# Attention and wave mixing on one core: k and v of three batches in nine-token runs, one batch's norms by square root, and a new order of the program

## The chip, the cores and the metric

The kernel runs on one core of one Trainium2 chip. Its engines work side by side, each through its own instructions in order: PE (matrix products, with PEld for the loading of the stationary operand), DVE (VectorE), ACT (ScalarE), POOL (GpSimd) and SP (SyncE, which here only issues transfers). DMA engines move data between device memory and the core's SBUF; products land in PSUM. The metric is the device time of one execution in microseconds, lower being better. A difference of less than 2% is counted as the same.

## The reference

Eight batches, eight heads, 576 tokens, 64 numbers a head; C = 512 channels.

```python
kv  = np.einsum('bhsd,bhse->bhde', k, v)          # a 64x64 matrix for each head
out = np.einsum('bhsd,bhde->bhse', q, kv)
rms = np.sqrt(np.mean(out * out, axis=-1, keepdims=True) + 1e-06)
x   = out / rms * g_norm                          # then heads side by side: (8, 576, 512)

theta  = x @ w_theta
zr, zi = x * np.cos(theta), x * np.sin(theta)
y = np.einsum('ts,bsd->btd', w_tok_r, zr) + np.einsum('ts,bsd->btd', w_tok_i, zi)
u = x + y
result = u + np.maximum(u @ w_ch, 0.0)
```

All inputs and the output are float32.

## The kernel before

**Tiling.** A batch's 576 tokens are four full tiles of 128 rows (token 4p + j on partition p for tile j, so that a partition's four tokens are one run in memory) and a tail of 64 tokens, in which two halves of the heads or channels share the 128 partitions. NT = 5 counts them, TL = 64 is the tail.

**Stages of a batch.** Names in brackets are those of tasks and tiles.

- k and v come in as float32, `kt` and `vt` [128, 8 heads, 5, 64], two buffers each (NKV = 2), by `heads_in` (runs of four tokens, 1 KB) and `tails_in` (single tokens, 256 bytes). q comes in over POOL as float16.
- `kv_piece` makes the kv matrices: for a pair of heads five steps, of 128 rows each, for either head. The first head's result stands on partitions 0 to 63 of a PSUM tile, the second's on 64 to 127. `kv_out` copies them into block-diagonal float16 tiles (`kbd`).
- q is transposed (`qps`, then a copy to `qT`; from batch 4 on by DMA) and multiplied with `kbd` (`raw`).
- The norm: `square` on ACT, `sums` on DVE (`ss`, the epsilon is in a ninth column of the tile), `root` on POOL (`rt`, the power -0.5), and `x_make` on DVE multiplies. Five of these chains make a batch, one for each tile.
- x is transposed (`xps`, a copy to `xD`), scaled by g (`xT`), and multiplied with the theta weight (`th`), which DVE has scaled by g beforehand (`wth`, in four pieces, `scale_theta`; `g` itself is scaled first).
- Sine and cosine: whole turns on ACT (`arg<-th`), the remainder on DVE, an absolute value on either, sine and cosine on ACT (`sc`), and z = x times both on DVE (`zm`, the tail in `zt`).
- The token mix (`y`, three parts for each of 2 x 4 blocks) uses `wT`, the two token weights transposed on PE in batch 0's time (`wps`, nine copies to `wT`). Then u (`um`, kept in the `wn` buffers), its transposes (`ups`, `us`, from batch 4 on by DMA), the channel mix (`v`), and the output (`fin`, `st`).

**What sets the order.** Nothing is scheduled while the program is built: every step is a task with a number, and `TURNS`, a table of numbers written out by hand, gives the order in which all tasks of all batches are emitted. A star takes the second engine of a task that may go to ACT or DVE; `r` and `a` stand for idle products on PE, which hold a PSUM buffer of their own. Each engine runs its share of the list in that order, and the framework adds the semaphores.

**Queues.** At the start SP issues k of batch 0, the tails of k of batch 1, g and the theta weight; ACT issues v of batch 0; POOL issues q and, behind a copy of one element of batch 0's k (`hold p`, into `gate`), the token weights. Later SP issues k and v of the other batches, the moves of z's tail, the transposes by DMA and the stores. A load of batch b into a buffer waits for the kv products of batch b - 2.

**Start of the program.** DVE fills constants and sets the unused half of each tail column to zero in all four k and v buffers. ACT loads its function table with one small sine (`warm`).

Of the kernel before, what the change touches and what calls it, by code (L numbers as in the profile page):

```python
# [32 lines left out]
0 6 39 4 3 1 31 46 r1 8 9 2 32 33* 40* 47* 24 11 10 5 a1 35 13 7 26 25 23 36 34* 48 49 37* 18 20 67  # L33
41 68 38 203 22 19 21 30 42 60 61* 50 204 51 53 62 r1 r1 54 55 63 56 43 44 57 58 12 14 52 17 64 r16
69 45 15 16 59 65 29 74 70 71 66 75 122 76 123 79 87 77 80 88 94 72 73 84 81 89 85 82* 90 91 95 96
a1 126 115 132 101 116 127 134 135* 92 93 28 133 128 102 108 138 129 98 86* 103 105 139 117 97 99
124 104* 125* 118 119 120 109 83* 239 240* a1 136 137 130 205 206 207 208 121 110 100 78* 131 106
107 225 140 148 211 112 210 209 226* 111 212* 141 152 232 164 165 153 113 114 142 213 201 198 200
199 154 218 149 150 227 166 214 143 215 202 216 151 167 228 219 229 230 520 27 155 217 231 168 169
170 233 144 383 384 145 156 157 220 369 146 246 370* 241 376 221 222 377* 171 147 223 247 242 243  # L40
224 158 363 248 259 249 260 261 159 364 234 235 365 262 236 263 366 264 368 390 391 250 361 360 244
362 237 172 173* 160 161 162 245 367* 163 238 177 178 371 266 372 192 193 385 251 252 386 267 174
253 373 265 374 175 387 388 256 273 254 257 274 268 375 269* 187 287 397 398 194 188 275 195 389 378
379 182 380 183* 358 356 515 359 357 514 517 516 280 392 270 288 289 393 394 271 281 277 276* 291
278 189 404 405* 381 184 521 382 399 522 555 190 282 556* 406 541 395 523 524 417 400 258 290* 292
407 525 526 255 418 283* 401 542* 527 402 518 185 272 396 293 403 179 528* 414 415* 419 279 529 409
410* 284 543 445 411 424 176 295 296 294 297 180 530 446 447 531 191 673 674 421 544 285 425 679 680
681 306 682 683 684 534 307 426 449 532 310 311 286 535* 308 302 428 545 685 675 186 412 420* 533
448 450 298 299 300 312 309 536 313 303 304 438 546 547 318 678 677 519 427* 429 416 557 562 301 319
548 320 305 431 537 538 563* 422 439 423 440 314 696 558 451 559 539 560 330 315 316 332 321 540 337  # L50
686 317 549 432 433 434 335 441* 442 443 331 333 687 322 323 324 326 327 328 688 430 336 325 561 435
436 689 676 329 564 697 575 698 565 350 690 550 338 345 582 351 347 340 551 576 699 552 444 346 583
341 413* 584 672 826 827 828 181 453 553 700 577 585 579 348 554 342 829 352 567 572 472 701 707 334
455 452 831 830 708 454 343 353 691 484 464 408* 437 578* 568 692 693 573 476 569 473 477 478 474
580 709 570 339 960 819 843 962 832 822 821 820 349 961 854 959 710 711 475 712 694 485 465 460 486
487 466 479 467 702 703 704 695 571 461 589 723 480 586 590 587 462 481 463 591 713 603 482 468 596
724 592 604 714 705 597 483 581 605 498 598 469 456 470 754 833 508 457 458 471 499* 706 607 606*
593 608 459 718 510 834 835 755 509 719 493 594 588 494 600 726 727 756 715 500 836 599 511 609 495
838 716 839 837 501 844 503 496 728 840 504* 595 729 845 601 846 841 733 966 734 967 740 968 969 505
488 735 842 730 731 741 970 971 847 720 855 848 638 639 630 631 849 742 856 758 566 489 717 344 613  # L60
736 757 732 574 721* 611 612 610 1099 1100 1101 1102 506 725* 602 642 1104 1103* 759 737 632 640 643
641 644 633 618 619 634 635 636 614 620 760 824 823 963 761 763 972 762 502 764 983 645 857 850 851
637 747 743 621 615 616 622 722 738 744 745 748 739 858 859 617 749 750* 626 627 751 752 656 628 623
624 625 661 490 629 753 746 973 657 974 852 975 491 853 781 785 769 646 786 770 782 787 783 765 984
766 767 976 964 825 788 977 662* 647 978 666 771 985 784 772 986 768 860 354 864 497 1105 862 507
196 797 355 994 197 866 987 867 868 663 894 664 773 774 789 775 873 895 896 988 870 979 865 898 897*
874 989 793 790 794 990 791 869 776 980 981 899 875 887 871 863 877 888 991 792 900 795 777 658 982
778 779 872 796 889 992 880 668 995 1000 799 901 665 492 798 902 904 876* 878 881 659 780 993 800
# [33 lines left out]
def kernel(  # L102
# [12 lines left out]
    nc = tc.nc  # L115
# [742 lines left out]
```

## Time and profile before

| | us |
|---|---|
| median of 3 runs | 225.27 |
| lowest and highest | 224.47 and 227.89 |
| the profiled execution's own time | 227.13 |
| its span, first to last instruction | 225.4 |
| first kv product on PE | 14.27 |
| first theta product on PE | 31.61 |
| last product ends, about | 220.9 |

The span is what the profile's rows are measured in; the execution's time has some 1.7 us around it. PE's busy time counts overlapping products once, so a busy PE need not be PE at its full pace: what an instruction costs a packed engine is better read from one start to the next. A transfer's time runs from its issue to the last byte's landing, queueing included.

### The profile page before, as it was taken

The numbers are of one execution on the slowest core, as the hardware profiler recorded it, in microseconds if no ns is written. First come the engines' busy times: TensorE is split into PE (matmuls) and PEld (weight loads), VectorE is DVE, ScalarE is ACT, GpSimd is POOL, SyncE is SP. The second block draws the span as 40 slices with busy tenths as digits, with TensorE's granted clock in tenths as the row PEclk, the third lists the DMA queues.
The fourth block names the chain that finished last, engine by engine and source line by source line (L and its number), as shares of the span: only waits on it lengthen the run. The fifth ranks groups of instructions, "written<-read, shape, count | busy, mean of one in ns | idle before, by whom it ended". The sixth has DMA issues, their size and how long they took to land.

```text
span 225.4 us, 5423 instructions
## 1 busy us (share of the span) xinstructions
PE 200.1 (89%) x2138; PEld 135.9 (60%) x2138; DVE 170.8 (76%) x350; ACT 144.7 (64%) x279; POOL 83.8 (37%) x78
## 2 busy tenths in 40 slices
PE   0147878999999999999999999999997999999991
PEld 0035335688755777666766578776655665755860
DVE  6006745777889969899598986889996999888562
ACT  2002447975699999975779798637998477258031
POOL 6080970007957617556151470453512501200000
PEclk9999979999999999999999999999999999999999
DMA  4999999996999399979599959579656884665424
GB/s 124 248 304 236 244 288 255 247 214 216 120 189 299 120 182 228 240 215 145 151 242 345 257 95 176 136 151 188 114 149 171 221 132 99 215 108 153 173 77 148
DMA packets 71721, 42.91 MB, mean 190 GB/s; under 512 B 38032, under 2 KB 67088, under 8 KB 71696
## 3 DMA queue, kind: packets, MB, share of 16 engines
q1 hardware_dynamic: 55680, 34.81, 60.8%
q0 software_dynamic: 14432, 6.57, 23.4%
q10 hardware_dynamic: 1584, 1.18, 1.7%
q8 instruction: 17, 0.28, 0.6%
q14 instruction: 8, 0.07, 0.1%
HBM read 33.06 MB, written 9.44 MB: 189 GB/s over the span
## 4 chain that ended last, share of the span: by engine, by line
PE 69%; DMA 12%; DVE 7%; ACT 6%; issue 2%; POOL 1%; SPq 1%; DVEq 0%
PE y L512 26%; PE th L420 11%; PE v L420 10%; PE kv L246 7%; DMA wn<-in_moe_w_tok_r_dram 7%; DMA kt<-in_k_dram 4%; PE raw L305 3%; PE xps L263 2%; PE th L423 2%; PE ups L263 2%; DVE ot L554 2%; DVE zm L489 1%; PE v L423 1%; PE qps L263 1%; DMA out_dram<-ot 1%
## 5 line engine op out<-in xcount | busy, mean ns | idle before, releaser
L343 POOL TENSOR_TENSOR rt<-ss,mhalf 128x8 f32<-128x8 f32 (+1 forms) x40 | 62.0, 1555 | 101.8 <-DVE ss L336 101.6
L512 PE MATMUL y<-wT,zm 128*128 128x256 f16 (+1 forms) x512 | 76.5, 286 | 0.7 <-DVE ot L554 0.6
L512 PEld LDWEIGHTS <-zm 128*128 128x128 f16 x512 | 47.9, 98 | 16.5 <-issue 1.6
L517 DVE SCALAR_TENSOR_TENSOR wn<-y,gcol,xT 128x320 f16<-128x320 f32 (+1 forms) x64 | 32.0, 513 | 8.1 <-PE y L512 7.4
L327 ACT ACTIVATE sqb<-raw 128x512 f32<-128x512 f32 x32 | 19.0, 596 | 28.2 <-PE raw L305 28.2
L420 PE MATMUL th<-wth,xD 128*128 128x512 f16 x128 | 34.0, 393 | 0.0
L420 PE MATMUL v<-wch,wn 128*128 128x512 f16 x128 | 31.7, 379 | 0.0
L436 ACT ACTIVATE arg<-th 128x512 f32<-128x512 f32 (+1 forms) x40 | 22.2, 555 | 14.5 <-PE th L420 8.1
L441 DVE SCALAR_TENSOR_TENSOR arg<-arg,th 128x512 f32<-128x512 f32 (+1 forms) x40 | 25.0, 630 | 7.6 <-ACT arg L436 7.3
L466 ACT ACTIVATE sc<-arg,quarter 128x512 f16<-128x512 f32 (+1 forms) x40 | 26.9, 674 | 0.8 <-DVE arg L451 0.7
L246 PE MATMUL kv<-vt,kt 128*64 128x64 f32 x640 | 23.3, 230 | 4.4 <-DMA vt<-in_v_dram 4.4
L246 PEld LDWEIGHTS kv<-vt,kt 128*64 128x64 f32 x640 | 21.0, 143 | 8.9 <-issue 3.7
L336 DVE TENSOR_REDUCE ss<-sqb 128x8 f32<-128x520 f32 x32 | 22.0, 689 | 4.5 <-ACT sqb L327 4.5
L459 ACT ACTIVATE sc<-arg 128x512 f16<-128x512 f32 (+1 forms) x40 | 23.0, 581 | 2.7 <-DVE zm L489 1.9
L353 DVE TENSOR_TENSOR x<-raw,rt 128x512 f16<-128x512 f32 x32 | 21.9, 685 | 2.3 <-POOL rt L343 2.3
L489 DVE TENSOR_TENSOR zm<-x,sc 128x1024 f16<-128x1024 f16 x32 | 21.8, 684 | 0.9 <-ACT sc L466 0.8
L512 PE MATMUL y<-wT,zt 128*128 128x256 f16 (+1 forms) x64 | 18.3, 286 | 0.6 <-DMA zt<-zf 0.6
L554 DVE SCALAR_TENSOR_TENSOR ot<-v,us 128x512 f32<-128x512 f32 (+1 forms) x28 | 16.8, 609 | 2.4 <-PE v L420 1.5
L420 PEld LDWEIGHTS <-wn 128*128 128x128 f16 x128 | 11.9, 98 | 10.9 <-issue 0.2
L405 ACT ACTIVATE xT<-xD,gcol 128x1024 f16<-128x1024 f16 (+1 forms) x18 | 16.6, 930 | 2.5 <-DMA xD<-x 2.5
L268 ACT COPY us<-ups 128x512 f16<-128x512 f16 (+1 forms) x20 | 10.5, 529 | 11.9 <-PE ups L263 8.2
L420 PEld LDWEIGHTS <-xD 128*128 128x128 f16 x128 | 11.9, 101 | 10.0 <-issue 1.9
(73 smaller groups left out, 227.1 us busy)
## 6 DMA issues: line engine op xcount, KB each, us to landing
out_dram<-ot SPq DMA_DIRECT2D x32, 256.0 KB, 2.8
vt<-in_v_dram SPq DMA_DIRECT2D x7, 1024.0 KB, 9.4
kt<-in_k_dram SPq DMA_DIRECT2D x7, 1024.0 KB, 8.2
qh<-in_q_dram POOLq DMA_DIRECT2D x7, 512.0 KB, 6.5
kt<-in_k_dram SPq DMA_DIRECT2D x2, 512.0 KB, 7.0
kt<-in_k_dram SPq DMA_DIRECT2D x8, 128.0 KB, 6.3
vt<-in_v_dram ACTq DMA_DIRECT2D x2, 512.0 KB, 14.0
zm<-in_moe_w_theta_dram SPq DMA_DIRECT2D x1, 1024.0 KB, 12.7
```

What stands on the lines that cost most here:

```text
L246: nc.tensor.matmul(t[i * D:(i + 1) * D, hp - lo, :], kt[b % NKV][:, 2 * hp + i, j, :], vt[b % NKV][:, 2 * hp + i, j, :], start=(j == 0), s ...
L336: nc.vector.reduce_sum(out=ss[:], in_=sq_sb.pop((b, j))[:], axis=AXX)
L343: nc.gpsimd.tensor_tensor(out=rt[:], in0=ss[:], in1=mhalf[:, 0:h], op=ALU.pow)
L353: nc.vector.tensor_tensor(out=x_pair[b, p][:, :, a * HC:(a + 1) * HC].rearrange("p t (h e) -> p h t e", e=D), in0=r[:].rearrange("p (h t e ...
L420: nc.tensor.matmul(t[:], piece(kc), w[:, kc, :], start=first, stop=last)
L436: nc.scalar.activation(out=arg[:, 1, :], in_=th_ps[b, j][:], func=AFT.Copy, bias=MAGIC)
L441: nc.vector.scalar_tensor_tensor(out=arg[:, 0, :], in0=arg[:, 1, :], scalar=MAGIC, in1=th_ps.pop((b, j))[:], op0=ALU.subtract, op1=ALU.sub ...
L459: nc.scalar.activation(out=sc[:, 0, :], in_=arg_sb[b, j][:, 0, :], func=AFT.Sin, bias=0.0, scale=-TURN * SHRINK,)
L466: nc.scalar.activation(out=sc_sb[b, j][:, 1, :], in_=arg_sb.pop((b, j))[:, 1, :], func=AFT.Sin, bias=quarter[:], scale=-TURN * SHRINK,)
L489: nc.vector.tensor_tensor(out=dst, in0=x.unsqueeze(1).broadcast_to((P, 2, w)), in1=sc[:], op=ALU.mult)
L512: nc.tensor.matmul(t[:, 0:hi - lo], s, wT[:, w, lo:hi], start=n == 0, stop=n == len(z) - 1)
L517: nc.vector.scalar_tensor_tensor(out=uTb[b % NUT][:, c, lo:hi], in0=y_ps.pop((b, h, c))[:, 0:hi - lo], scalar=gcol[:, 0:1], in1=xTb[b % NX ...
```

## The change

Three things change together.

**k and v of batches 0 to 2 (NINE = 3) come in nine-token runs.** 576 tokens are 64 runs of nine tokens (RUN = 9), 2304 bytes each. Even heads stand on partitions 0 to 63, odd ones on 64 to 127 (`runs_in`, one transfer for each half i). So a head's kv sum has nine steps of 64 rows in place of five of 128: 72 products a batch for 40. The tail's loads and its cleared rows go away for these batches; for the first two batches in the other form, 3 and 4, the rows are cleared later, by `kz`, on POOL or DVE. Batch 0's k and v come in four transfers each.

**Batch 0's norms (RS = (0,)) go by square root.** ACT takes the root of the sums (`square_root`) and DVE its reciprocal, in place of POOL's power. ACT's first table load is for the square root, and a second (`load_sine`) follows after the last root.

**`TURNS` is new**, for the whole program: order, engines, and 14 idle products for 22.

```diff
@@ TURNS
-0 6 39 4 3 1 31 46 r1 8 9 2 32 33* 40* 47* 24 11 10 5 a1 35 13 7 26 25 23 36 34* 48 49 37* 18 20 67
+1 3 0 2 8 4 13 a1 15 12 6 5 33 34 41 7 9 49 37 36* 42 35 43 44 38 50* 51 52 a4 57 14 19 18 17 45 16
...
+    NINE = 3
+    RS = (0,)
-    kt = [const.tile([P, H, NT, D], FP32, name=f"kt{i}") for i in range(NKV)]
+    kt = [const.tile([P, H * NT * D], FP32, name=f"kt{i}") for i in range(NKV)]
...
+    RUN = S // TL
+    def runs_of(t):
+        return t[:, 0:NHP * RUN * D].rearrange("p (m e) -> p m e", m=NHP)
...
+    def runs_in(eng, dst, src, b, i, lo, hi):
+        eng.dma_start(
+            out=runs_of(dst)[i * TL:(i + 1) * TL, lo:hi, :],
+            in_=src[b].rearrange("(m i) (p j) d -> i p m (j d)", i=2, j=RUN)[i, :, lo:hi, :],
+        )
+    def clear_tails(i, eng):
+        e = nc.vector if eng == "DVE" else nc.gpsimd
+        for t in (kt[i], vt[i]):
+            e.memset(t[TL:P, H * NJ * D:H * NT * D], 0.0)
...
     def kv_piece(b, hp, lo, n):
...
-        for j in range(NT):
+        kb, vb = kt[b % NKV], vt[b % NKV]
+        n = RUN if b < NINE else NT
+        for j in range(n):
             for i in range(2):
+                if b < NINE:
+                    half = slice(i * TL, (i + 1) * TL)
+                    ks, vs = (runs_of(x)[half, hp, j * D:(j + 1) * D] for x in (kb, vb))
...
                 nc.tensor.matmul(
-                    t[i * D:(i + 1) * D, hp - lo, :],
-                    kt[b % NKV][:, 2 * hp + i, j, :],
-                    vt[b % NKV][:, 2 * hp + i, j, :],
-                    start=(j == 0), stop=(j == NT - 1),
+                    t[i * D:(i + 1) * D, hp - lo, :], ks, vs, start=(j == 0), stop=(j == n - 1)
                 )
...
     def root(b, j):
...
-        nc.gpsimd.tensor_tensor(out=rt[:], in0=ss[:], in1=mhalf[:, 0:h], op=ALU.pow)
+        if b in RS:
+            nc.vector.reciprocal(out=rt[:], in_=rs_sb.pop((b, j))[:])
+        else:
+            nc.gpsimd.tensor_tensor(out=rt[:], in0=ss[:], in1=mhalf[:, 0:h], op=ALU.pow)
...
+    def square_root(b, j):
+        ss = sq_sb[b, j]
+        rs = work.tile(list(ss.shape), FP32, tag="rs" + ("" if full(j) else "e"),
+                       bufs=4 if full(j) else 1, name="rs")
+        nc.scalar.activation(out=rs[:], in_=ss[:], func=AFT.Sqrt)
+        rs_sb[b, j] = rs
+    def load_sine():
+        nc.scalar.activation(out=warm[:], in_=quarter[:], func=AFT.Sin)
...
-    hold = add("hold p", "POOL", lambda: hold_pool(kt[0][0:1, H - 1, 0, 0:1]), [kb])
+    hold = add("hold p", "POOL", lambda: hold_pool(kt[0][0:1, 3 * RUN * D:3 * RUN * D + 1]), k0[1])
...
+        if NINE <= b < NINE + NKV:
+            k_.append(add(f"kz {b}", "POOL|DVE", lambda e: clear_tails(b % NKV, e), old))
...
+        if b == 0:
+            sine_ready = add("warm", "ACT", load_sine, of("rs", 0))
...
-        nc.scalar.activation(out=warm[:], in_=quarter[:], func=AFT.Sin)
-        for i in range(NKV):
-            nc.vector.memset(kt[i][TL:P, :, NJ, :], 0.0)
-            nc.vector.memset(vt[i][TL:P, :, NJ, :], 0.0)
+        nc.scalar.activation(out=warm[:], in_=quarter[:], func=AFT.Sqrt)
```

How the order moves is shown at three places. In the rows below a name with a number is one buffer (`kt_64` is k's first, `kt_65` its second, `vt_66` and `vt_67` are v's, `zm_77` first holds the theta weight), and x2 means two of the kind in a row.

The first is SP's queue at the start of the program, before:

```order
L181 DMA kt_64<-in_k_dram 128x4x256
L187 DMA kt_64<-in_k_dram 64x8x64
L181 DMA kt_64<-in_k_dram 128x4x256
L187 DMA kt_65<-in_k_dram 64x8x64
L219 DMA gcol<-in_g_norm_dram 64x1 x2
L213 DMA zm_77<-in_moe_w_theta_dram 128x4x512
L187 DMA vt_67<-in_v_dram 64x8x64
L181 DMA vt_67<-in_v_dram 128x8x256
L181 DMA kt_65<-in_k_dram 128x8x256
```

And the same place after:

```order
L207 DMA kt_64<-in_k_dram 64x2x576 x4
L244 DMA gcol<-in_g_norm_dram 64x1
L238 DMA zm_77<-in_moe_w_theta_dram 128x4x512
L244 DMA gcol<-in_g_norm_dram 64x1
L207 DMA kt_65<-in_k_dram 64x4x576
L207 DMA vt_67<-in_v_dram 64x4x576 x2
L207 DMA kt_65<-in_k_dram 64x4x576
L195 DMA vt_67<-in_v_dram 128x8x256
L207 DMA vt_66<-in_v_dram 64x4x576
L207 DMA kt_64<-in_k_dram 64x4x576
```

The theta weight stands right behind batch 0's k, with half of g on either side of it; v of batch 3 (the 128x8x256 row, into the buffer of batch 1) stands ahead of v and k of batch 2.

The second is DVE in the first batch's norms, from the copies of the kv matrices on, before:

```order
L270 COPY qT<-qps 128x512
L336 TENSOR_REDUCE ss<-sqb_92 128x8
L336 TENSOR_REDUCE ss<-sqb_93 128x8
L336 TENSOR_REDUCE ss<-sqb_92 128x8
L225 TENSOR_SCALAR gcol<-gcol 128x1
L230 TENSOR_SCALAR wth<-zm_77,gcol 128x512
L353 TENSOR_TENSOR x<-raw,rt 128x4x2x64
L230 TENSOR_SCALAR wth<-zm_77,gcol 128x512
L336 TENSOR_REDUCE ss<-sqb_91 128x8
L353 TENSOR_TENSOR x<-raw,rt 128x4x2x64
```

And after:

```order
L301 COPY qT<-qps 128x512
L250 TENSOR_SCALAR gcol<-gcol 128x1
L255 TENSOR_SCALAR wth<-zm_77,gcol 128x512 x3
L367 TENSOR_REDUCE ss<-sqb_92 128x8
L255 TENSOR_SCALAR wth<-zm_77,gcol 128x512
L301 CAST kbd_74<-kv 64x2x64 x2
L367 TENSOR_REDUCE ss<-sqb_93 128x8
L375 RECIPROCAL rt<-rs 128x8
L399 TENSOR_TENSOR x<-raw,rt 128x4x2x64
L375 RECIPROCAL rt<-rs 128x8
L301 COPY qT<-qps 128x512
L367 TENSOR_REDUCE ss<-sqb_91 128x8
```

The scaling of g and of three pieces of the theta weight moved ahead of the first sum, and reciprocals stand between the sums and x.

The third is ACT from the last root to the first weight copy, after the change:

```order
L386 ACTIVATE rs<-ss 128x4
L482 ACTIVATE arg<-th 128x512
L299 COPY xD<-xps 128x256
L482 ACTIVATE arg<-th 128x512
L390 ACT_TABLE_LOAD
L390 ACTIVATE warm<-quarter 128x1
L505 ACTIVATE sc<-arg 128x512 x2
L512 ACTIVATE sc<-arg,quarter 128x512
L482 ACTIVATE arg<-th 128x512
L299 COPY wT<-wps 128x576
```

Before, the same stretch of ACT was:

```order
L436 ACTIVATE arg<-th 128x512
L268 COPY xD<-xps 128x256
L459 ACTIVATE sc<-arg 128x512
L436 ACTIVATE arg<-th 128x512
L436 ACTIVATE arg<-th 128x256
L268 COPY wT<-wps 128x576
L466 ACTIVATE sc<-arg,quarter 128x512
L268 COPY wT<-wps 128x576
```

The second table load stands between the whole turns of batch 0's second tile and its first sine. Of the nine copies of the turned token weights ACT makes four (seven before). Over the whole program DVE has 18 copies of kv matrices (10 before), 12 full copies of transposed u and none of half width (5 and 3 before), 12 of transposed x (6), 11 scalings by g (6), 5 weight copies (2) and 4 copies of transposed q (12), each taken from or given to ACT.

More of the change, by code (lines that the diff above doesn't have):

```diff
@@ L692 @@
             ss = add(f"ss{w} {b} {j}", "DVE", lambda b=b, j=j: sums(b, j), [sq], [("ss" + w, 4)])
-            rt = add(f"rt{w} {b} {j}", "POOL", lambda b=b, j=j: root(b, j), [ss], [("rt" + w, 4)])
+            rs = ss
+            if b in RS:
+                rs = add(f"rs{w} {b} {j}", "ACT", lambda b=b, j=j: square_root(b, j), [ss])
+                last["rs", b, j] = rs
+            rt = add(f"rt{w} {b} {j}", "DVE" if b in RS else "POOL", lambda b=b, j=j: root(b, j), [rs],
+                     [("rt" + w, 4)])
             new = not full(j) or a == 0
@@ L739 @@
             ab = add(f"ab{w} {b} {j}", "DVE|ACT", lambda e, b=b, j=j: even_arg(b, j, e), [ar])
[L740 removed]
+            si = add(f"si{w} {b} {j}", "ACT", lambda b=b, j=j: sine(b, j), [ar, sine_ready],
+                     [("sc" + w, 2)])
             co = add(f"co{w} {b} {j}", "ACT", lambda b=b, j=j: cosine(b, j), [ab, si])
```

147 lines of the change are left out of this document (85 added, 62 removed), and 9 rows, old and new, of the table TURNS.

## The prediction, as it was made before the changed kernel ran

> **What bounds the kernel now.** I read the page first: busy time, the span in 40 slices, the chain that ended last.
>
> ```profile
> span 225.4 us, 5423 instructions
> PE 200.1 (89%) x2138; PEld 135.9 (60%) x2138; DVE 170.8 (76%) x350; ACT 144.7 (64%) x279; POOL 83.8 (37%) x78
> PE   0147878999999999999999999999997999999991
> PE 69%; DMA 12%; DVE 7%; ACT 6%; issue 2%; POOL 1%; SPq 1%; DVEq 0%
> ```
>
> PE is full from the eighth slice on, at about 45 us, and 69% of the chain is its own work. So there are two levers: when PE gets full, and how much work it holds from then on. The busy times by stage (columns: stretch, its length, then PE, PEld, DVE, ACT, POOL busy with counts, granted clock, DMA share, GB/s), with two short DMA stretches, say what fills the start.
>
> ```profile
> 0.00:14.20 14.20, 0.60 (x4) 0.34 (x4) 3.47 (x13) 1.49 (x2) 5.75 (x16) 1.00 0.93 204
> 14.20:31.60 17.40, 13.28 (x155) 8.75 (x156) 10.38 (x24) 5.57 (x12) 11.30 (x11) 0.99 1.20 268
> 31.60:50.00 18.40, 17.23 (x198) 11.63 (x196) 11.03 (x26) 14.27 (x29) 1.12 (x2) 0.92 1.16 238
> 150.00:180.00 30.00, 28.83 (x232) 18.09 (x230) 27.13 (x55) 22.26 (x41) 12.60 (x10) 1.00 0.77 166
> 2.00:4.00 2.00, 0.00 (x0) 0.00 (x0) 1.68 (x5) 0.23 (x2) 2.00 (x4) 1.00 0.81 259
> 14.00:20.00 6.00, 4.53 (x72) 3.59 (x74) 1.91 (x6) 0.00 (x0) 2.70 (x4) 1.00 1.20 289
> ```
>
> Until 14.2 PE has 0.6 us of work: it waits for loads. The third row's clock of 0.92 over 18.4 us is about 1.5 us of PE's pace lost, and ACT is busy 14.27 of 18.4 there. The timeline gives the milestones.
>
> ```profile
> 8.48 0.38 SPq L213 DMA_DIRECT2D zm<-in_moe_w_theta_dram  x1
> 12.13 0.17 POOL L222 COPY gate<-kt 1x1 f32<-1x1 f32 x1 [7.75 <-DMA kt<-in_k_dram]
> 14.27 1.33 PE L246 MATMUL kv<-vt,kt 128*64 128x64 f32 x20 [3.24 <-DMA vt<-in_v_dram]
> 19.24 1.39 PE L246 MATMUL kv<-vt,kt 128*64 128x64 f32 x40 [1.20 <-DMA vt<-in_v_dram]
> 21.89 0.68 DVE L336 TENSOR_REDUCE ss<-sqb 128x8 f32<-128x520 f32 x1
> 22.73 6.50 POOL L343 TENSOR_TENSOR rt<-ss,mhalf 128x8 f32<-128x8 f32 x4 [6.03 <-DVE ss L336]
> 25.43 0.48 DVE L230 TENSOR_SCALAR wth<-zm,gcol 128x512 f16<-128x512 f32 x1
> 25.83 0.68 DVE L353 TENSOR_TENSOR x<-raw,rt 128x512 f16<-128x512 f32 x1
> 28.81 0.69 DVE L353 TENSOR_TENSOR x<-raw,rt 128x512 f16<-128x512 f32 x1
> 29.41 0.42 DVE L336 TENSOR_REDUCE ss<-sqe 128x4 f32<-128x260 f32 x1
> 31.61 3.33 PE L420 MATMUL th<-wth,xD 128*128 128x512 f16 x8
> 49.93 0.27 PE L512 MATMUL y<-wT,zt 128*128 128x256 f16 x1
> zm<-in_moe_w_theta_dram SPq DMA_DIRECT2D x1, 1024.0 KB, 12.7
> ```
>
> First kv product 14.27, first sum of squares 21.89, first theta product 31.61, first product with batch 0's last z (zt) 49.93. I follow the change through these.
>
> **The loads.** Batch 0's k and v are 2.36 MB before and after, in fewer and longer runs. SP's queue now holds k (1.18 MB) and then the theta weight (1.05), ACT's holds v (1.18), POOL's q (0.52 as landed). SP sends the upper halves first and ACT the lower ones, so the first kv product needs three quarters of both: 1.77 MB and about 0.35 MB of q beside it. By 4.0 us 0.52 MB are in (259 GB/s for 2 us); at the 289 GB/s of 14 to 20 us the rest takes 5.5 us. With half a microsecond to land, kv starts near 10.0. The weight lies behind it all: 4.2 MB with the first tokens, so 4.0 + 3.7/0.289 = 16.7 at 289 GB/s and nearer 15.5 if longer runs go faster; I take 16.5 where it now lands at 8.48 + 12.7 = 21.2. The tokens' gate, now 12.13, comes earlier too and hides behind that.
>
> **The kv products.** A head's sum goes from five steps of 128 rows to nine of 64, two heads side by side: 144 matmul records in a batch for 80.
>
> ```profile
> 43.79 2.55 PE L246 MATMUL kv<-vt,kt 128*64 128x64 f32 x80
> 46.27 0.40 PE L263 MATMUL qps<-ident,qh 128*128 128x128 f16 x4
> 68.42 0.56 PE th L423 x8
> 70.30 0.86 PE th L420 x4
> ```
>
> 80 records take 46.27 - 43.79 = 2.48 us, 31 ns each, so 64 more are 2.0 us a batch. That holds if two row halves run side by side as two column halves do now: eight half-width products of 256 columns take 0.56 us, four of 512, the same columns, 0.86. No row shows row halves; the bounds are 31 and, one after the other, 62 ns. I take 31, as both keep their own columns. Batch 0's extra 2.0 us falls in the start: 72 records at the cold pace of the row at 14.27 (about 53 ns after its latency) are 3.8 us, so the first half ends near 13.9. q's transposes and the second half's first piece (36 records) stand before the first raw product; with its square the first sum could start at 17.0. But DVE now scales g and three pieces of the theta weight ahead of it, so it waits for the weight: 16.5, 0.14 for g (its row is below) and three pieces at 0.40, 17.8. That is 4.1 us earlier than 21.89.
>
> **Square root for power.** From the first sum to theta it takes 9.7 us now, as four powers on POOL take 6.50 us in a row. After, a root on ACT and a reciprocal on DVE stand between. Neither is in the trace. For the durations:
>
> ```profile
> L436 ACT ACTIVATE arg<-th 128x512 f32<-128x512 f32 x32 | 19.1, 598 | 8.4 <-PE th L420 8.1
> L459 ACT ACTIVATE sc<-arg 128x512 f16<-128x512 f32 x32 | 19.9, 624 | 2.7 <-DVE zm L489 1.9 <-DVE arg L441 0.8
> L466 ACT ACTIVATE sc<-arg,quarter 128x512 f16<-128x512 f32 x32 | 23.0, 718 | 0.7 <-DVE arg L451 0.7
> L268 ACT COPY wT<-wps 128x576 f16<-128x576 f16 x7 | 4.4, 638 | 0.7 <-PE wps L584 0.6
> L268 ACT CAST kbd<-kv 64x256 f16<-64x256 f32 x24 | 8.8, 366 | 3.0 <-PE kv L246 2.7
> L441 DVE SCALAR_TENSOR_TENSOR arg<-arg,th 128x512 f32<-128x512 f32 x32 | 21.8, 684 | 7.0 <-ACT arg L436 6.6
> L489 DVE TENSOR_TENSOR zm<-x,sc 128x1024 f16<-128x1024 f16 x32 | 21.8, 684 | 0.9 <-ACT sc L466 0.8
> L823 ACT ACT_TABLE_LOAD x1 | 1.3, 1283 | 0.7 <-PEq L842 0.7
> L823 ACT ACTIVATE warm<-quarter 128x1 f32<-128x1 f32 x1 | 0.2, 203 | 0.0
> L225 DVE TENSOR_SCALAR gcol<-gcol 128x1 f32<-128x1 f32 x1 | 0.1, 144 | 0.0
> L270 DVE CAST kbd<-kv 64x256 f16<-64x256 f32 x4 | 1.7, 421 | 1.8 <-ACT kbd L268 1.7
> L270 DVE COPY us<-ups 128x512 f16<-128x512 f16 x5 | 2.1, 417 | 0.2 <-PE ups L263 0.2
> ```
>
> A root of 8 columns lies between 0.20 (one column) and 0.60 (512); the reciprocal between 0.14 and 0.42. I take 0.2 and 0.15, the rows of one column being nearest. DVE is then the path, in its own order: three sums and three x at 0.60 from start to start (28.81 to 29.41), a weight piece at 0.40 (25.43 to 25.83), two casts 0.5, three reciprocals 0.45, a copy 0.35: 5.3 us. Transposes, their copy and the hops add 1.2. Theta starts 17.8 + 6.5 = 24.3, against 31.61: **-7.3**. With the upper ends of both prices it is 25.4; with the weight at 15.5 it is 23.3.
>
> **Theta to the first zt product.** Now 18.3 us. After, ACT's row up to the last cosine is 15.3 us: five each of the three activations above (4 at full width: 7.8, the half ones 1.3), four weight copies 2.6, two q copies, an x copy and an absolute value 2.2, the second table load with its warm-up 1.5. Three weight copies and four casts go over to DVE, which has 14.7 us there by the same counting and so stays beside ACT. PE needs 15.7 us of products there at full clock, the longer kv among them, and hides too. ACT starts 1.2 after theta and z follows 0.7 behind the cosine: 17.7 with half a microsecond of gaps, **-0.6**. Bounds: 15.7 if ACT isn't waited for, 19.5 if the clock drops again.
>
> The table load is one more than before, 1.28 us in its row. The Trainium skill, ScalarE: Activation LUTs (What ACT_TABLE_LOAD costs), gives 1283 ns and a drain of 1380 ns for every change of set. Its first figure is this trace's; by its sum this stage would be 1.4 us longer, 221.2 in the end. The trace's load has nothing ahead of it, so it cannot show a drain.
>
> **The rest.** From 49.93 on the same products stand in another order, with batch 2's 64 records: **+2.0**. ACT gives casts and copies to DVE over the whole run: 10 casts at 0.42, 7 u copies and 4 x copies at 0.42, 3 weight copies and 5 scalings, less 8 q copies: some 8 us more on DVE. DVE was busy 27.13 of 30 from 150 to 180, the one long stretch where it could lead; a tenth of the run at that density makes **+0.6** (0 if PE covers it all, 8 if none). Two memsets that go to POOL hide before batch 1's powers. On SP batch 2's loads stand behind v of batch 3, which waits for batch 1's products: out at about 36.7, 3.4 MB at 268 GB/s, in at 49.9, needed near 53; 3 us are left. The last store is a half tile: **-0.2**.
>
> Sum: -7.3 - 0.6 + 2.0 + 0.6 - 0.2 = -5.5 us: span 225.4 to 219.9. The profiled execution took 227.13 with what lies around its span, so 221.6; it stood 1.86 above the median of 225.27. For the median I predict **219.8**.
>
> **Rivals.** (1) Row halves take turns. Both heads write one accumulator tile, from different row halves. Then 288 records of batches 1 and 2 cost 31 ns more, 8.9 us, and the start 2.5: 231.2, slower than before. It decides from about 16 ns a record. For it: no row shows row halves together. Against: the column halves do run together, and these keep them. The Trainium skill, TensorEngine Tiling (Array Packing), Gotcha 1, says that different row tiles cannot access the same PSUM bank simultaneously; that is this rival, and no run here shows it yet. Chance 0.09. (2) The theta weight lands no earlier than now, 21.2: DVE's first sum waits behind it to 22.5, theta starts 29.0, and 4.7 us are lost: 224.5. For it: the DMA share is above 1.1 all along, and DVE's order puts the weight first. Against: some 2,500 runs fewer ahead of it (of k and v: 3,584 now, 1,024 after). Chance 0.17. (3) DVE becomes the pace in the middle: half of its 8 us show, 223.8. For it: 27.13 of 30; against: PE's row reads 9 there too. Chance 0.14. My forecast holds the rest, 0.60, alone between 217.3 and 222.
>
> **Numbers.** Range 217.0 to 225.5: it holds the forecast and rivals 2 and 3, and leaves out rival 1 and the ends. Two per cent is about what a measurement of this kernel tells from no change: below 220.8 is faster. Faster: four fifths of the forecast and a little of rival 2 and 3, 0.51. Slower: most of rival 1, 0.07. Same: the rest, 0.42.
>
> **What would show it.** First kv near 10, first sum near 17.8 right behind the weight, theta near 24.3, first zt product near 42; kv pairs at 31 ns a record; no power on POOL in batch 0; a second table load of 1.28 us. The forecast fails if kv records take over 45 ns, if DVE's first sum waits past 20, or if PE shows gaps behind DVE after 50.

## The result, and the profile after

| | before | after |
|---|---|---|
| median, beside each other | 225.39 us (4 runs, 224.47 to 227.89) | 232.49 us (4 runs, 231.75 to 232.88) |
| ratio after to before, 95% interval | | 1.0325 (1.0281 to 1.0370) |
| the profiled execution, and its span | 227.13, 225.4 | 232.56, 230.8 |

The changed kernel is slower, by 7 us. From its page: the span, the busy times, PE's row of 40 slices, and the chain that ended last by engine.

```profile
span 230.8 us, 5784 instructions
PE 203.4 (88%) x2322; PEld 141.5 (61%) x2322; DVE 176.9 (77%) x370; ACT 138.6 (60%) x269; POOL 77.5 (34%) x75
PE   1049588999889999999999999999997999999992
PE 56%; DMA 25%; DVE 6%; ACT 5%; POOL 3%; SPq 2%; issue 1%; DVEq 0%; POOLq 0%; ACTq 0%
```

PE's busy time grew by 3.3 us, but its part of the chain fell from 69% to 56%, and that of transfers rose from 12% to 25%. So the new time is waiting for data. The timeline has the milestones that the prediction named (columns: start, length, engine, line, operation; in brackets the idle time before it and what ended it).

```profile
11.48 0.44 PE L280 MATMUL kv<-vt,kt 64*64 64x64 f32 x2 [9.44 <-DMA kt<-in_k_dram]
13.80 0.17 POOL L247 COPY gate<-kt 1x1 f32<-1x1 f32 x1 [10.65 <-DMA kt<-in_k_dram]
15.20 3.88 PE L280 MATMUL kv<-vt,kt 64*64 64x64 f32 x70 [3.28 <-DMA vt<-in_v_dram]
22.10 0.15 DVE L250 TENSOR_SCALAR gcol<-gcol 128x1 f32<-128x1 f32 x1 [1.93 <-DMA gcol<-in_g_norm_dram]
23.48 0.69 DVE L367 TENSOR_REDUCE ss<-sqb 128x8 f32<-128x520 f32 x1
30.56 1.90 PE L466 MATMUL th<-wth,xD 128*128 128x512 f16 x8
37.09 0.39 PE L629 MATMUL wps<-ident,wn 128*128 128x128 f16 x4 [1.04 <-DMA wn<-in_moe_w_tok_r_dram]
50.31 0.30 PE L558 MATMUL y<-wT,zt 128*128 128x320 f16 x1
63.10 1.23 PE L280 MATMUL kv<-vt,kt 64*64 64x64 f32 x34 [0.96 <-DMA kt<-in_k_dram]
```

kv starts at 11.48, with two records, and goes on only at 15.20. The scaling of g waits to 22.10, the first sum stands behind it at 23.48 (21.89 before), and theta starts at 30.56, only 1 us earlier than before. Up to the first sum everything waited for a transfer. The busy times by stretch say why (last two columns: share of the DMA engines' time, GB/s; the row from 6 to 14 us is of the kernel before), and the list of issues how long single transfers took (the last number is from issue to landing).

```profile
2.00:4.00 2.00, 0.04 (x1) 0.00 (x0) 0.50 (x2) 0.22 (x2) 1.15 (x2) 1.00 0.77 198
4.00:12.00 8.00, 0.44 (x2) 0.28 (x2) 0.00 (x0) 0.00 (x0) 0.00 (x0) 1.00 1.12 220
53.00:56.00 3.00, 2.70 (x31) 2.22 (x29) 2.61 (x5) 1.04 (x3) 1.41 (x1) 1.00 1.04 217
6.00:14.00 8.00, 0.60 (x4) 0.34 (x4) 0.00 (x0) 0.00 (x0) 1.87 (x5) 1.00 1.24 263
zm<-in_moe_w_theta_dram SPq DMA_DIRECT2D x1, 1024.0 KB, 16.7
kt<-in_k_dram SPq DMA_DIRECT2D x4, 576.0 KB, 14.5
wn<-in_moe_w_tok_r_dram POOLq DMA_DIRECT2D x1, 576.0 KB, 20.5
```

The DMA engines are fully taken (share 1.04 to 1.12) and yet move 217 to 220 GB/s. Stretch for stretch that is a step back from the shorter runs of before: 236 GB/s for 263 from 6 to 14 us, 262 for 289 from 14 to 20. From 53 to 56 us SP's transfers of batch 2 were alone, and their packets of 2304 bytes took 179 ns each (median over the trace's packets). In the kernel before SP's and ACT's packets of 1024 bytes took 46 to 59 ns (medians from 4 to 12 us), so 104 to 133 would go with the size. The longer runs were there, but each took 1.3 to 1.7 times that. The theta weight needed 16.7 us for 12.7 (issued at 4.82, it landed at 21.5, no earlier than the 21.2 of before), the second token weights 20.5 (15.2 before).

### The profile page after: what moved, and what is told of

The parts are those of the page before. It is cut to its first block, busy times and chain, and to the rows that moved or that the text cites. A ratio compares the mean times of both kernels' runs of the same rounds, so it can differ in the third digit from the quotient of the medians.

```text
span 230.8 us, 5784 instructions
## 1 busy us (share of the span) xinstructions
PE 203.4 (88%) x2322; PEld 141.5 (61%) x2322; DVE 176.9 (77%) x370; ACT 138.6 (60%) x269; POOL 77.5 (34%) x75
## 4 chain that ended last, share of the span: by engine, by line
PE 56%; DMA 25%; DVE 6%; ACT 5%; POOL 3%; SPq 2%; issue 1%; DVEq 0%; POOLq 0%; ACTq 0%
PE y L558 20%; DMA kt<-in_k_dram 12%; PE v L466 10%; PE th L466 9%; DMA wn<-in_moe_w_tok_r_dram 9%; PE kv L280 7%; DMA xD<-x 5%; POOL rt L377 2%; SPq L207 2%; PE raw L336 2%; PE xps L294 2%; PE ups L294 1%; PE th L469 1%; PE v L469 1%; DVE ot L600 1%
## 5 line engine op out<-in xcount | busy, mean ns | idle before, releaser
L377 POOL TENSOR_TENSOR rt<-ss,mhalf 128x8 f32<-128x8 f32 (+1 forms) x35 | 54.5, 1559 | 97.7 <-DVE ss L367 95.0
L558 PE MATMUL y<-wT,zm 128*128 128x320 f16 (+1 forms) x512 | 75.6, 286 | 0.0
L280 PE MATMUL kv<-vt,kt 64*64 64x64 f32 (+1 forms) x832 | 30.9, 230 | 14.4 <-DMA kt<-in_k_dram 10.4
L280 PEld LDWEIGHTS kv<-vt,kt 64*64 64x64 f32 (+1 forms) x832 | 28.0, 143 | 17.9 <-DMA vt<-in_v_dram 10.0
L563 DVE SCALAR_TENSOR_TENSOR wn<-y,gcol,xT 128x320 f16<-128x320 f32 (+1 forms) x64 | 31.5, 512 | 5.2 <-PE y L558 4.8
L466 PE MATMUL th<-wth,xD 128*128 128x512 f16 x128 | 32.2, 380 | 1.9 <-DMA xD<-x 1.8
L482 ACT ACTIVATE arg<-th 128x512 f32<-128x512 f32 (+1 forms) x40 | 21.7, 554 | 14.4 <-PE th L466 11.9
L301 DVE CAST kbd<-kv 64x256 f16<-64x256 f32 (+1 forms) x18 | 7.1, 392 | 21.7 <-PE kv L280 19.7
L299 ACT COPY qT<-qps 128x512 f16<-128x512 f16 (+1 forms) x16 | 8.8, 548 | 20.6 <-PE qps L294 20.6
L466 PEld LDWEIGHTS <-xD 128*128 128x128 f16 x128 | 11.1, 98 | 13.8 <-DMA xD<-x 2.5
L558 PE MATMUL y<-wT,zt 128*128 128x320 f16 (+1 forms) x64 | 18.3, 286 | 0.0
```

Of the source, the lines that this page charges most:

```text
L280: nc.tensor.matmul(t[i * D:(i + 1) * D, hp - lo, :], ks, vs, start=(j == 0), stop=(j == n - 1))
L377: nc.gpsimd.tensor_tensor(out=rt[:], in0=ss[:], in1=mhalf[:, 0:h], op=ALU.pow)
L466: nc.tensor.matmul(t[:], piece(kc), w[:, kc, :], start=first, stop=last)
L482: nc.scalar.activation(out=arg[:, 1, :], in_=th_ps[b, j][:], func=AFT.Copy, bias=MAGIC)
L558: nc.tensor.matmul(t[:, 0:hi - lo], s, wT[:, w, lo:hi], start=n == 0, stop=n == len(z) - 1)
L563: nc.vector.scalar_tensor_tensor(out=uTb[b % NUT][:, c, lo:hi], in0=y_ps.pop((b, h, c))[:, 0:hi - lo], scalar=gcol[:, 0:1], in1=xTb[b % NX ...
```

## The experiments

Each was timed beside the kernel before on the same chip; ratios are to that. The table has the milestones of each profiled execution in us: first kv product, first sum, first theta product, first product with zt, and from there to the end of PE's last product.

| kernel | kv | sum | theta | zt | zt to end | median | ratio (95%) |
|---|---|---|---|---|---|---|---|
| before | 14.27 | 21.89 | 31.61 | 49.93 | 170.8 | 225.27 | |
| after | 11.48 | 23.48 | 30.56 | 50.31 | 176.2 | 232.49 | 1.0325 (1.0281 to 1.0370) |
| e1_whole | 8.19 | 18.10 | 25.18 | 43.86 | 173.6 | 223.62 | 0.9921 (0.9867 to 0.9975) |
| e6_pairs | 7.70 | 17.38 | 24.45 | 43.23 | 174.3 | 223.80 | 0.9925 (0.9895 to 0.9955) |
| e11_stepped | 12.96 | 20.05 | 27.14 | 45.81 | 173.2 | 225.17 | 0.9973 (0.9944 to 1.0001) |
| e5_halves | 12.58 | 19.64 | 31.83 | 50.05 | 170.9 | 227.60 | 1.0108 (1.0002 to 1.0214) |
| e9_v3_later | 11.27 | 23.07 | 30.15 | 55.98 | 173.8 | 236.27 | 1.0477 (1.0430 to 1.0525) |
| e8_old_order | 14.69 | 23.10 | 38.02 | 58.15 | 173.4 | 236.12 | 1.0482 (1.0420 to 1.0543) |
| e12_order_alone | 10.81 | 21.45 | 29.50 | 50.40 | 171.6 | 228.25 | 1.0124 (1.0088 to 1.0160) |
| e2_root | 13.63 | 20.50 | 32.32 | 51.10 | 169.9 | 227.01 | 1.0082 (1.0031 to 1.0133) |
| e3_power | 11.86 | 21.38 | 32.69 | 62.70 | 175.8 | 244.53 | 1.0863 (1.0721 to 1.1006) |
| e7_five_steps | 8.39 | 16.42 | 23.50 | 48.54 | 173.2 | 227.42 | 1.0074 (1.0044 to 1.0105) |
| e10_nine_two | 8.36 | 17.69 | 24.76 | 43.60 | 171.9 | 223.00 | 0.9883 (0.9832 to 0.9934) |
| e13_pairs_in_order | 7.42 | 18.11 | 26.39 | 45.06 | 171.9 | 222.66 | 0.9830 (0.9793 to 0.9867) |

### Why the transfers were slow

The suspicion: each transfer of nine-token runs goes to a closed half of the partitions, 0 to 63 or 64 to 127. First, the two halves of each pair of transfers were joined into one over all 128.

```diff
-            out=runs_of(dst)[i * TL:(i + 1) * TL, lo:hi, :],
-            in_=src[b].rearrange("(m i) (p j) d -> i p m (j d)", i=2, j=RUN)[i, :, lo:hi, :],
+            out=runs_of(dst)[:, lo:hi, :],
+            in_=src[b].rearrange("h s d -> (h s d)").rearrange("(m q e) -> q m e", m=NHP, q=P)[:, lo:hi, :],
...
```

> The changed kernel, but each pair of nine-token transfers (one to partitions 0 to 63, one to 64 to 127) is one transfer over all 128 partitions: same bytes, same 2304-byte runs, same order. Theory A, transfers to half of the partitions are the slow thing: packets of 2304 bytes fall from about 170 ns to about 100, the first kv products come near 11.5 instead of 15.2 us, theta near 26 instead of 30.6, batch 2's k and v are in before PE wants them (no wait near 62), and the time is 224 to 226. Theory B, the long runs themselves are slow, or 2304 bytes are an awkward length: packets stay above 150 ns and the time above 230. Theory C, the new order is at fault behind the start: packets get faster and theta earlier, but the time stays at 229 or more.

The time fell from 232.49 to 223.62, a little below theory A's range. That also halves the number of transfers, so a second version keeps their number and size and gives each one half of the head pairs, on all partitions:

```diff
+        n = (hi - lo) // 2
+        at = slice(lo + i * n, lo + i * n + n)
-            out=runs_of(dst)[i * TL:(i + 1) * TL, lo:hi, :],
+            out=runs_of(dst)[:, at, :],
...
```

> The changed kernel with as many transfers of the same size, but each of them brings half of the head pairs to all 128 partitions instead of all pairs to 64 partitions. Theory A (a transfer to 64 partitions is held to about 215 GB/s, whatever its run length): 2304-byte packets at 95 to 105 ns, SP alone near 390 GB/s, first kv product before 9 us, time 222.5 to 225.0 as with whole transfers. Theory B (twice as many transfers, or the order in which they stand, made the start slow): packets stay near 170 ns, first kv product near 11.5, time 230 to 233.

223.80, the same. Two stretches of this kernel, for the first 8 us of full load and for the one in which SP's batch 2 stands alone:

```profile
4.00:12.00 8.00, 2.96 (x50) 2.78 (x52) 0.00 (x0) 0.00 (x0) 2.13 (x5) 1.00 1.11 317
44.00:47.00 3.00, 3.00 (x31) 2.44 (x30) 2.94 (x6) 1.33 (x3) 2.98 (x2) 1.00 1.04 393
```

At the same DMA share of 1.04 the transfers move 393 GB/s, where the halves moved 217; a packet takes 93 ns. So not the number of transfers, but where they go. A third version leaves 64 partitions to a transfer, but every second one of the 128:

```diff
-            out=runs_of(dst)[i * TL:(i + 1) * TL, lo:hi, :],
-            in_=src[b].rearrange("(m i) (p j) d -> i p m (j d)", i=2, j=RUN)[i, :, lo:hi, :],
+            out=runs_of(dst)[i:P:2, lo:hi, :],
+            in_=src[b].rearrange("h s d -> (h s d)").rearrange("(m p i e) -> i p m e", m=NHP, p=TL, i=2)[i, :, lo:hi, :],
```

> The changed kernel with the same number and size of transfers, each still to 64 partitions, but to every second one of the 128 (runs dealt out one by one) instead of a closed half. Theory A (the cap of about 215 GB/s belongs to the half 0 to 63 or 64 to 127, whose way into the memory is half as wide): 2304-byte packets at 95 to 105 ns, first kv product before 9 us, time 223 to 225.5. Theory B (the cap belongs to the number of partitions, 64 in a transfer, or to the number of runs that a transfer hands each DMA engine): packets near 170 ns, time 230 to 233.

```profile
4.00:6.00 2.00, 0.00 (x0) 0.00 (x0) 0.00 (x0) 0.00 (x0) 0.00 (x0) 1.00 0.95 195
8.00:10.00 2.00, 0.00 (x0) 0.00 (x0) 0.00 (x0) 0.00 (x0) 0.00 (x0) 1.00 1.11 331
44.00:47.00 3.00, 3.00 (x31) 2.40 (x29) 2.86 (x8) 1.95 (x4) 0.40 (x1) 1.00 1.05 397
```

397 GB/s with 64 partitions a transfer: the cap belongs to the closed half, not to the count. The first 6 us ran slowly here as well (195 GB/s from 4 to 6 us, although a packet took 93 to 106 ns in the median), and kv started at 12.96 and not before 9. Why is open; the rest is as theory A had it. The Trainium skill, SBUF — State Buffer (Door 1: The DMA port swizzle), gives the way in as 16 ports, of which partitions 0 to 63 reach eight, with an asymptote of about 218 GB/s for 64 partitions: the trace's 217 agrees. The Trainium skill, SBUF — State Buffer ("Can I just issue two DMAs to hit both halves?"), says that two transfers at once, one to each half, gain only 6% over one. No run here tests that. SP takes the upper half first and ACT the lower, but ACT's first packet landed only at 4.7 us, and by the count of packets SP had filled the upper half at 6.9 and went on in the lower one, which ACT left at 11.1. So from 6.9 to 11.1 us both queues wrote partitions 0 to 63, at 223 GB/s with POOL's q; only from 11.1 to 12.9 were they on opposite halves, at 258, too short a stretch to tell. The same section of the Trainium skill has one transfer spanning all 128 partitions as the only way to all ports; every second partition, from 0 to 127, was enough here, at 397 GB/s.

The reverse, halves in the kernel before with its 1 KB runs:

```diff
-        eng.dma_start(
-            out=dst[:, hs, 0:NJ, :],
...
+        for ps_ in ((slice(0, TL), slice(TL, P)) if b < 3 else (slice(0, P),)):
+            eng.dma_start(
+                out=dst[ps_, hs, 0:NJ, :],
...
```

> The kernel before, but the four-token runs of k and v of batches 0 to 2 (1024 bytes) go in two transfers each, to partitions 0 to 63 and 64 to 127. Theory A (half of the partitions is slow): their packets go from about 47 to 59 ns to 80 to 110, the first kv product from 14.3 to 17 us or later, the time to 228 to 231. Theory B (run length): packets as before, and 225 to 227.

Neither theory: 227.60 is below theory A's range and above theory B's, and the first kv product came earlier (12.58), not later. The ratio, 1.0108, has its interval just above one and is inside the 2% that count as the same. From 29 to 32 us this kernel (first row) moved 248 GB/s, the one before (second row) 313:

```profile
29.00:32.00 3.00, 1.88 (x14) 1.44 (x15) 0.14 (x1) 1.13 (x2) 1.47 (x2) 0.50 1.24 248
29.00:32.00 3.00, 2.00 (x16) 1.35 (x17) 1.85 (x4) 1.86 (x4) 2.93 (x5) 0.85 1.23 313
```

From 20 to 28 us, however, the two moved the same (236 and 235), and SP's 1 KB packets rose only from 57 to 63 ns on average up to 60 us, less than theory A said. The clock granted to PE from 29 to 32 us differs too, 0.50 for 0.85 (the column ahead of the share), so a loss of 1% cannot be put down to the transfers alone. Why 1 KB runs lose so much less in halves than 2304-byte runs is open.

### What the late loads of batch 2 cost

v of batch 3 stands ahead of batch 2's loads in SP's queue. One number of the table was moved:

```diff
-161 385 366 208 206 209 207 239 ...
+161 385 208 206 209 207 366 239 ...
```

> The changed kernel with one number of the table moved: v of batch 3 stands behind the four loads of batch 2 in SP's queue instead of ahead of them. Theory A (batch 2's loads were late because they stood behind a load that waits for batch 1's products): they go out at about 36, batch 2's kv products no longer wait, the 3 us lost between 60 and 70 us come back: 229 to 230. Theory B (at half rate they would have landed late in any case, or the late part is not what counts): 231.5 to 233.

Both theories fell: 236.27, slower than the changed kernel, and the loads went out at 22 us, not at 36.

```profile
40.87 0.59 PE L629 MATMUL wps<-ident,wn 128*128 128x128 f16 x4 [5.23 <-DMA wn<-in_moe_w_tok_r_dram]
55.98 0.30 PE L558 MATMUL y<-wT,zt 128*128 128x320 f16 x1
```

From zt to the end it takes 173.8 us, 2.4 less than the changed kernel: batch 2's wait was worth about that, near the 3 us of theory A. But batch 2's 2.36 MB now go out at 22 us beside the token weights, which land for PE at 40.87 in place of 37.09, and zt moves from 50.31 to 55.98. From 23 to 40 us all transfers together made 245 to 259 GB/s with the DMA engines' share at 1.12 to 1.13, so an earlier transfer made another later. Behind v of batch 3 batch 2 was out of the token weights' way. The token weights account for 3.8 us of zt's 5.7. The granted clock of PE comes on top: 0.93 from 30 to 40 us and 0.73 from 40 to 50, where the changed kernel had 1.00, so PE lost the pace of 0.7 + 2.7 = 3.4 us.

The other variants have such a loss too, and their times contain it. Worked out in the same way from 20 to 50 us, PE lost the pace of 1.7 us in the kernel before, e2_root and e12_order_alone, 3.4 in e5_halves and e7_five_steps, 5.1 in e8_old_order and 6.8 in e3_power. The changed kernel, e1_whole, e6_pairs, e10_nine_two, e11_stepped and e13_pairs_in_order had a granted clock of 1.00 throughout these 30 us.

### The order, the root and the loads, one without the other

The old order and the power, with nine-token runs of batches 0 to 2 over all partitions:

```diff
...
+                k_ += [add(f"load {n}{b}", "SP", lambda t=t, src=src: runs_in(nc.sync, t, src, b, 0, NHP), old),
...
```

> The kernel before, in its old order and with the power on POOL, with k and v of batches 0 to 2 in nine-token runs over all 128 partitions. Theory A (the faster loads give the gain by themselves): first kv product near 8.5, first theta product near 26.5, 5 us early, less 3.7 us for the extra records of batches 1 and 2: 223 to 225. Theory B (the old order holds theta behind the token weights and the powers whatever the loads do): theta at 30 or later, time 227 to 230.

```profile
14.16 0.60 PE L293 MATMUL qps<-ident,qh 128*128 128x128 f16 x4 [14.16 <-DMA qh<-in_q_dram]
36.13 0.61 PE L628 MATMUL wps<-ident,wn 128*128 128x128 f16 x4 [5.39 <-DMA wn<-in_moe_w_tok_r_dram]
38.02 2.34 PE L465 MATMUL th<-wth,xD 128*128 128x512 f16 x5
```

Slower than either theory, 236.12. k and v are there early, but PE's old order starts with q's transposes, and POOL's q now comes in beside the long packets, at 14.16. The token weights follow late, and in the old order theta stands behind them. The new order alone, with the loads of before:

```diff
-    NINE = 3
+    NINE = 0
...
```

> The changed kernel's order and its square root, with k and v of all batches loaded as before (runs of four tokens and single tail tokens, five steps). Theory A (the new order needs the loads to be early): first kv product near 13 to 14, first theta product 28 to 30, batch 1's kv waits for its tails near 35 as with five steps in batches 1 and 2, first product with zt near 51, time 227 to 231. Theory B (the new order and the root are the gain and the load form adds only records): 224 or less.

Theory A: 228.25. First kv is earlier than theory A had it, 10.81, but theta comes at 29.50 and batch 1's kv waits for k to 36.69. The root alone, in the old order:

```diff
-        nc.gpsimd.tensor_tensor(out=rt[:], in0=ss[:], in1=mhalf[:, 0:h], op=ALU.pow)
+        if b == 0:
+            rs = work.tile([P, h], FP32, tag="rs" + e, bufs=1 if e else 4, name="rs")
+            nc.scalar.activation(out=rs[:], in_=ss[:], func=AFT.Sqrt)
+            nc.vector.reciprocal(out=rt[:], in_=rs[:])
...
```

> The kernel before with batch 0's norms by root and reciprocal, in its old order. If the root pays: theta starts near 28.5 to 29.5 instead of 31.6, and the time is 222.5 to 224.5. If not (the theta weight or ACT is the next to wait for): 225 to 227, with the second table load of 1.28 us in ACT's fullest stretch.

227.01, no gain: theta starts at 32.32, since the token weights' transposes stand ahead of it there. And the changed kernel with POOL's power in place of the root:

```diff
-        if b in RS:
-            nc.vector.reciprocal(out=rt[:], in_=rs_sb.pop((b, j))[:])
-        else:
-            nc.gpsimd.tensor_tensor(out=rt[:], in0=ss[:], in1=mhalf[:, 0:h], op=ALU.pow)
+        nc.gpsimd.tensor_tensor(out=rt[:], in0=ss[:], in1=mhalf[:, 0:h], op=ALU.pow)
...
```

> The changed kernel with batch 0's norms by POOL's power again (no root, no reciprocal, one table load). If the root pays as forecast: theta starts 2 to 4 us later than 30.6 and the time is 234 to 237, more where POOL's transfers stand ahead of the powers. If the start is set by the loads alone: theta within 1 us of 30.6 and 232 to 233.

```profile
22.22 3.39 POOL L374 TENSOR_TENSOR rt<-ss,mhalf 128x8 f32<-128x8 f32 x2 [19.07 <-DVE ss L367]
27.63 0.17 POOL L247 COPY gate<-kt 1x1 f32<-1x1 f32 x1
30.33 0.74 POOL L230 DMA_DIRECT2D wn<-in_moe_w_tok_r_dram  x1
```

244.53, above both expectations: the powers take the root's place in the list, ahead of the gate, so POOL issues the token weights at 30 in place of 16, and zt goes to 62.70. This prices the new order without the root, not the power itself. In these runs the three parts of the change lean on each other: the order needs the root off POOL, and loads that arrive; the loads need an order that takes k and v first.

### The kv records, and the best version

Batches 1 and 2 in five steps (their tails cleared ahead of the loads), the rest as with whole transfers:

```diff
-    NINE = 3
+    NINE = 1
...
```

> The changed kernel with whole transfers, and only batch 0 in nine-token runs: batches 1 and 2 come in runs of four tokens and take 80 kv records each instead of 144. Theory A (the 64 extra records of a batch cost PE 29 ns each and nothing hides them): 128 records, 3.7 us less than whole transfers' 223.6, so 219.5 to 220.5. Theory B (the shorter runs of batches 1 and 2 land later than needed, or PE was waiting anyway): 222.5 or more, with waits of kv for k or v before 70 us.

```profile
32.48 1.12 PE L286 MATMUL kv<-vt,kt 128*64 128x64 f32 x16 [4.69 <-issue]
34.77 0.48 PE L286 MATMUL kv<-vt,kt 128*64 128x64 f32 x4 [1.17 <-DMA kt<-in_k_dram]
```

227.42, theory B: in this order batch 1's kv products stand before 30 us, and its shorter runs and tails are not there yet; PE idles 5.9 us ahead of the 20 records (for the first 4.69 the profile names nothing that was waited for). So batch 1 wants the long runs, and only batch 2 was put back, with the half-pair transfers:

```diff
-    NINE = 3
+    NINE = 2
...
```

> The half-pairs version (every transfer to all 128 partitions), with batch 2 in runs of four tokens and five steps, batches 0 and 1 in nine-token runs. Theory A (batch 2's 64 extra records are paid by PE at 29 ns each, and only batch 1's loads need the long runs): 1.9 us less than 223.8, so 221.5 to 222.3. Theory B (batch 2's loads in short runs land after PE needs them at 55 us, as batch 1's did in the run before): 223.5 or more, with a wait of kv for k or v between 50 and 62 us.

PE's last product ends at 215.46, against 217.48 with nine steps: 2.0 us for 64 records, as priced, and batch 2's kv products at 55 us show no wait for k or v. The median moved less, to 223.00, between the ranges of the two theories. Last, this version with batch 0's loads, kv products and first sums in another order:

```diff
-1 3 0 2 8 4 13 a1 15 12 6 5 33 34 41 7 9 49 37 36* 42 ...
+0 1 2 3 8 4 13 a1 12 15 5 6 7 33 34 37 41 9 49 38 36* 42 ...
-57 14 19 18 17 45 16 39* 53 46 40 58 65 59 54 47 48 60 ...
+57 45 39* 53 46 40 58 65 59 54 47 48 14 19 18 17 16 60 ...
```

> The version with batch 2 in five steps (223.0), with the start put in the order in which full-width transfers land: batch 0's pairs 0, 1, 2, 3 on SP and on ACT, g whole ahead of the theta weight, kv pairs 0 to 2 ahead of q's transposes, the first two sums and the first x ahead of the scaling of g and the weight. Theory A (the start is held by the order of the loads and by DVE's first sum standing behind the weight): first sum near 15, first theta product 22.5 to 23.5 against 24.8, time 221 to 222. Theory B (theta waits for the scaled weight, which lands near 16 whatever stands ahead): first theta product stays at 24 to 25, time 222.5 to 223.5.

Neither theory: the time, 222.66, is one that theory B allowed, but theta came at 26.39, later than both had it.

```profile
10.48 4.10 PE L282 MATMUL kv<-vt,kt 64*64 64x64 f32 x72 [0.88 <-DMA vt<-in_v_dram]
14.52 1.04 PE L296 MATMUL qps<-ident,qh 128*128 128x128 f16 x8
18.11 0.69 DVE L369 TENSOR_REDUCE ss<-sqb 128x8 f32<-128x520 f32 x1 [2.09 <-ACT sqb L360]
20.92 1.98 DVE L257 TENSOR_SCALAR wth<-zm,gcol 128x512 f16<-128x512 f32 x4
```

The 72 records take 57 ns each here, so they hold q's transposes to 14.52, the first sum is no earlier, and the weight's scaling now stands between the sums: theta starts at 26.39. It is the best measured of all, ratio 0.983 (0.9793 to 0.9867), but whether that is more than 2% stays unclear, and these runs don't tell it apart from e10_nine_two.

## Why the prediction was wrong, point by point

Forecast 219.8, measured 232.49: outside the range. The spans differ by 230.8 - 219.9 = 10.9 us, and the milestones place them: theta at 30.56 for 24.3, +6.3; theta to zt 19.75 for 17.7, +2.0; zt to PE's end 176.2 for the 173.4 that +2.0 and +0.6 make of 170.8, +2.8.

**The loads: this step failed.** "At the 289 GB/s of 14 to 20 us the rest takes 5.5 us" took a rate from transfers that spread over all partitions, and gave it to transfers that fill a half: from 4 to 12 us they made 220. The prediction asked how long the runs were, not where they land. It let SP begin with the upper half and ACT with the lower, and yet from 6.9 to 11.1 us both were in the lower. Its own sign of failure came true: a first sum past 20. First kv was 11.48, with the bulk at 15.20, for 10.0; the first half of kv ended at 19.08 for 13.9; the weight's scaling began at 22.29 for 16.6. With the same bytes at full width (e6_pairs) the later steps come in near the forecast: g scaled at 15.99 and the weight at 16.18, the first sum right behind three pieces of it at 17.38 for 17.8, and theta at 24.45 for 24.3. There the loads were faster than forecast (first kv 7.70, for 10.0; the weight in at 15.6, for 16.5; 300 to 319 GB/s from 6 to 20 us), and from the first sum to theta it took 7.1 us for 6.5, so the two errors cancel and theta's close agreement is in part luck.

**Rival 2** was the nearest in kind, and its condition came true: the weight landed at 21.5, no earlier than before, and g's second half, behind it in the queue, held the scaling to 22.10. Its remark that the DMA share is above 1.1 all along overlooks the 0.93 of the first 14.2 us. And it put the weight alone at risk and stopped at 224.5. The same rate also made batch 1's, the tokens' and batch 2's loads late.

**kv side by side: right, by its pace.** Rival 1's 231.2 is near the measured time, for another reason: the records did not take turns.

```profile
38.05 1.26 PE L280 MATMUL kv<-vt,kt 64*64 64x64 f32 x36
39.25 1.04 PE L466 MATMUL th<-wth,xD 128*128 128x512 f16 x4
```

36 records in 39.25 - 38.05 = 1.20 us are 33 ns each, for 31 forecast and 62 if they took turns. The rule cited for rival 1 (the Trainium skill, TensorEngine Tiling (Array Packing), Gotcha 1) is not borne out for two row halves that write their own partitions of one accumulator.

**The root: right.** Rows of 0.21 us for a root and 0.19 for a reciprocal answer to 0.2 and 0.15; from the first sum to theta it took 7.1 us, for 6.5 forecast and 9.7 before.

```profile
24.20 0.21 ACT L386 ACTIVATE rs<-ss 128x8 f32<-128x8 f32 x1 [0.89 <-DVE ss L367]
25.60 0.19 DVE L375 RECIPROCAL rt<-rs 128x8 f32<-128x8 f32 x1
32.87 0.60 ACT L482 ACTIVATE arg<-th 128x512 f32<-128x512 f32 x1
33.50 1.28 ACT L390 ACT_TABLE_LOAD   x1
34.79 0.20 ACT L390 ACTIVATE warm<-quarter 128x1 f32<-128x1 f32 x1
```

The second table load took 1.28 us with work right ahead of it and right behind it: the drain of 1380 ns that the Trainium skill, ScalarE: Activation LUTs (What ACT_TABLE_LOAD costs), adds to a load does not show here.

**Theta to zt, -0.6: not there.** 19.75 in the changed kernel, where PE waits for the token weights to 37.09; that wait is 1.04 us. At full width the stage is still 18.8, 0.5 more than before, and there the path was wrong: the prediction had ACT as the pace and 15.7 us of PE's products hidden beside it. ACT was busy 15.60 us of the stage, near the 15.3 forecast; PE was busy 18.59 of 18.8, with no wait in its rows, at a granted clock of 1.00. Which of PE's terms was too small is open.

**"3 us are left" for batch 2's loads: failed.** They were issued at 44 to 47, since batch 1's products were late, and at half the rate: the chain shows k of batch 2 on its way from 47.13 to PE's start at 63.10.

```profile
47.13 15.83 DMA kt<-in_k_dram
172.39 5.61 DMA xD<-x
```

**The rest, +2.6.** At full width zt to the end took 173.6 (e1_whole) and 174.3 (e6_pairs), 2.8 and 3.4 more than before, for 2.6: about right. The changed kernel's further 2 us or so are batch 2's wait (e9_v3_later gained 2.4; PE's own rows show 0.96 and 0.76 us of idling at these products) and, less surely, turned x by DMA at 172, whose wait no experiment took away. Rival 3, DVE as the pace, was not tested by itself; at full width the measured 2.8 to 3.4 leave 0.2 to 0.8 us for it beyond the forecast's 0.6.

Against the kernel before, full width is worth 0.75% and not the 2.4% forecast. In the milestones e6_pairs gains 3.3 us at PE's end (217.48 for 220.76); the rest of the forecast's gain was the -0.6 that did not come, the larger late part, and a profiled execution of before that was 1.9 us over its median.

## What to carry to other kernels

Read a transfer's rate together with the partitions that it writes: here 64 partitions of a closed half got 217 GB/s and all 128, or every second one, 393 to 397. Two queues meant for opposite halves ended up in the same one for 4.2 us, because one of them started late. When a layout stands on half the partitions, let one transfer fill both halves, or give each transfer fewer items on all of them. And when transfers are the bound, moving one ahead only moves the wait: price it by who lands later.

## What was not expected of the hardware

- A transfer's rate at a full DMA share went from 217 to 393 GB/s by the choice of partitions alone, with the same runs, sizes and number of transfers.
- What POOL's queue brings landed later beside long packets on SP and ACT: batch 0's q took 12.4 us to land in e6_pairs and 15.7 in e8_old_order for 11.7 before, the second token weights 17.4 and 21.7 for 15.2. That the length is the cause isn't shown: the token weights took 20.2 in e7_five_steps as well, where only batch 0 has long packets.
- PE's granted clock fell between 20 and 50 us in eight of the fourteen kernels, the one before among them, and cost the pace of 1.7 to 6.8 us. What sets it off was not tested.
- kv records at the start of the program, on an engine that had been idle, took 55 ns (70 in 3.88 us) and later 33, at a granted clock of 1.00 in both stretches.
